# Which DRAM rows go to which partition: x and the output of a pre-LN block dealt four rows to a partition in four groups, in place of sixteen to a partition

## The chip, the cores and the metric

The kernel runs on one core of one Trainium2 chip. Its time is the device time in microseconds (us) of one execution. Engines are named as in the profile: PE is TensorE (matmuls; PEld its weight loads), DVE is VectorE, ACT is ScalarE, POOL is GpSimd, and SP is SyncE, whose queue (SPq) issues every DMA of this kernel. A core's DMAs are spread over 16 DMA engines.

## The reference

A transformer block with layer norms ahead of its two halves: linear attention with 32 heads of 16, then a dense layer with ReLU. S = 2048 rows, D = 512, Dff = 1792, all in bf16. Cut to what matters:

```python
def _A_ref(x, wqkv, wo):                       # 32 heads of 16
    q, k, v = split_heads(x @ wqkv)
    phi = lambda t: jnp.where(t > 0, t + 1, jnp.exp(t)) + 1e-6
    pq, pk = phi(q), phi(k)
    kv  = jnp.einsum("bhsd,bhse->bhde", pk, v)      # sum over all rows s
    z   = jnp.einsum("bhsd->bhd", pk)               # sum over all rows s
    num = jnp.einsum("bhqd,bhde->bhqe", pq, kv)
    den = jnp.einsum("bhqd,bhd->bhq", pq, z)[..., None] + 1e-6
    return join_heads(num / den) @ wo

def _B_ref(x, w1, w2):
    return jnp.maximum(x @ w1, 0) @ w2

h  = x + _A_ref(_layernorm(x), wqkv, wo)
h2 = h + _B_ref(_layernorm(h), w1, w2)
```

Every step works on each row by itself, but for `kv` and `z`, which are sums over all rows. No step looks at the order of the rows.

## The kernel before, in words

The 2048 rows stand on 128 partitions, 16 rows to each: the tile `x_nat` is [128, 16, 512], and its middle index t (0 to 15) is called a row tile here. Row tile t holds one row of every partition. Four row tiles make a chunk of 512 columns for the transposed operands (`CT` = 4, `NCH` = 4 chunks).

Which row of x is on which partition is said in one place, line 94, by the view `x_v = xf.rearrange("(p t) d -> p t d", p=P)`: partition p holds rows 16p to 16p + 15. Line 95 gives the output the same view, `of_v`. Three small functions use them:

- `op_lx(t, n)` (L200, its DMA is L201) loads n row tiles from t on: for each partition n rows of 1 KB, contiguous in DRAM. One such DMA is 128 KB for n = 1, 256 KB for n = 2 and 512 KB for n = 4.
- `load_d` (L203, its DMA is L204) loads the weights; `op_lk` loads two of the four blocks of wk (256 KB), `op_l1` two of the four blocks of w1 (896 KB).
- `op_fd(t, k, w)` (L527, its DMA is L529) stores row tile t of the result, 128 KB, from one of the four buffers of `o_t`; the last row tile is stored in three pieces of 32 KB, 64 KB and 32 KB.

The order of all work is written out by hand in the string `ORDER`: some 540 words such as `lx.4.2`, each of which calls `op_lx(4, 2)`. Each engine, and the SP queue, runs its instructions in the order in which these words emit them. The loads at the start stand there in the order lx.0.1, lx.2.1, lx.1.1, lx.3.1, lk.0.2, lx.4.2, lk.2.2, lx.6.2, lx.8.4, lx.12.4.

The words around the start are these. `S.t` (L222) takes the statistics of row tile t on DVE as soon as its x has landed; `A` (L223) and `R` (ACT, L228 and L229) make mean and 1/std of them; `N.t` (DVE, L247) writes the normalized row tile into `h_nat`. `T` and `E` transpose a row tile by PE (L266) and copy it into `lnT` on ACT (L276); later row tiles are transposed by DMA, `X.t` (L287). `K.t` (PE, L295) multiplies `lnT` by wk; `F` (ACT exp, L313), `U` (ACT ReLU, L316), `M` (DVE, L320) and `D` (DVE, L323) turn the product into phi(k), in the tile `pk_lo` for t = 0 and 1 and in `at` for the others. `G.t` (PE, L347) adds the row tile's share of ln(x) transposed times phi(k), from which `kv` is made, into four PSUM banks. `Q` (PE, L303) makes q. `warm` (L215) are matmuls on zeros ahead of the first real work.

After the sums over all rows are complete comes the long part: `dn` and `dt` make 1/den (`dt` by DMA transposes, L464), `h` (PE, L478) the attention output, `p` (PE, L494) the product with w1, `f` (PE, L514) that with w2, `fo` (DVE, L522) the final sum into `o_t`, and `fd` stores it.

On DVE the words after the first statistics run ... S.6, M.0.1, N.5, N.4, S.7, D.0.1, M.1.1 ...: an engine that waits for its next word's input does not pass it by.

Of the kernel before, what the change touches and what calls it, by code (L numbers as in the profile page):

```python
# [56 lines left out]
def kernel(  # L57
# [10 lines left out]
    nc = tc.nc  # L68
    P = 128
    xf = A_x.flatten_outer_dims()  # L70
    of = out.flatten_outer_dims()
# [6 lines left out]
    CT = CW // P  # L78
# [7 lines left out]
    NO = 4  # L86
# [4 lines left out]

    ctx.enter_context(tc.manual_schedule())

    x_v = xf.rearrange("(p t) d -> p t d", p=P)
    of_v = of.rearrange("(p t) d -> p t d", p=P)
    wqkv_v = A_wqkv.rearrange("(k p) n -> p k n", p=P)
    wo_v = A_wo.rearrange("(k p) n -> p k n", p=P)
    w1_v = B_w1.rearrange("(k p) n -> p k n", p=P)
# [2 lines left out]
    x_nat = big.tile([P, NT, D], BF16, name="x_nat")  # L101
# [38 lines left out]
    o_t = gT  # L140
# [57 lines left out]


    def op_lx(t, n):  # L200
        nc.sync.dma_start(out=x_nat[:, t : t + n, :], in_=x_v[:, t : t + n, :])  # L201

    def load_d(dst, src, k, n):  # L203
        nc.sync.dma_start(out=dst[:, k : k + n, :], in_=src[:, k : k + n, :])  # L204
# [321 lines left out]

    def op_fd(t, k=0, w=KD):  # L527
        cols = slice(k * P, (k + w) * P)
        nc.sync.dma_start(out=of_v[:, t, cols], in_=o_t[:, t % NO, cols])  # L529

    ops = {k[3:]: v for k, v in locals().items() if k.startswith("op_")}
    for word in ORDER.split():
# [32 lines left out]
```

## Time and profile before

| | |
|---|---|
| time, median of 3 runs | 170.41 us (170.3 to 171.33) |
| profiled execution, its own time | 172.11 us |
| its span, first to last instruction | 170.4 us |
| granted TensorE clock | 1.000 |
| busy: PE, DVE, ACT, POOL | 162.6, 106.0, 62.8, 4.8 us |
| moved by DMA | 15.87 MB in 32234 packets |
| HBM read, written | 7.86 MB, 2.10 MB |

The profile is one execution, recorded by the hardware profiler; times in it count from the span's start. Busy time is the time in which an engine executes something; in "idle before" the profile names what an engine waited for. The chain of waits follows the work that ended last back to the start, at each step to what released it. The DMA share is the busy time of the 16 DMA engines' packets over 16 times the window, and can pass 1 where packets overlap on an engine. A DMA's time to landing runs from its issue to the last byte's arrival.

### The profile page before, as it was taken

How to read it: one execution, taken by the hardware profiler on the slowest of the kernel's cores; microseconds unless marked ns; L12 is line 12 of the kernel's file. 1: busy time of each engine (PE TensorE's matmuls, PEld its weight loads, DVE VectorE, ACT ScalarE, POOL GpSimd, SP SyncE). 2: the span in 40 equal slices, each digit the busy share in tenths (PEclk: the TensorE clock that was granted, in tenths of full speed). 3: DMA queues.
4: the chain of work that ended last, by engine and by line, in shares of the span. 5: the costliest groups of instructions: out<-in, count | busy, mean ns of one | idle time of the engine just before them, and what ended most of it. 6: DMA issues, size and time to landing. Idle time of an engine off the chain costs nothing.

```text
span 170.4 us, 2280 instructions
## 1 busy us (share of the span) xinstructions
PE 162.6 (95%) x859; PEld 75.4 (44%) x859; DVE 106.0 (62%) x208; ACT 62.8 (37%) x94; POOL 4.8 (3%) x21
## 2 busy tenths in 40 slices
PE   7679989999989999999999999999999999999993
PEld 2234434445534355444444444444444444444552
DVE  3969999896768999736673983860453060315251
ACT  3768776882978857272000202034001002030000
POOL 7400000000000000000000000000000000000000
PEclk9999999999999999999999999999999999999999
DMA  4956555793353555457252142114000020000202
GB/s 125 278 213 149 99 96 123 221 392 95 73 56 62 103 93 209 88 157 185 49 82 62 20 103 62 31 36 91 0 31 0 0 92 4 31 0 19 81 31 85
DMA packets 32234, 15.87 MB, mean 93 GB/s; under 512 B 24800, under 2 KB 31200, under 8 KB 32224
## 3 DMA queue, kind: packets, MB, share of 16 engines
q1 hardware_dynamic: 32224, 15.74, 36.6%
q8 instruction: 6, 0.10, 0.2%
q14 instruction: 4, 0.03, 0.1%
HBM read 7.86 MB, written 2.10 MB: 58 GB/s over the span
## 4 chain that ended last, share of the span: by engine, by line
PE 81%; DMA 7%; DVE 5%; SPq 3%; issue 1%; ACT 1%; DVEq 0%
PE bk L494 28%; PE bk L514 28%; PE bk L478 8%; PE bk L347 6%; PE bk L303 6%; PE bk L295 4%; DMA x_nat<-in_A_x_dram 4%; DMA lnT<-h_nat 2%; DVE st L222 2%; SPq L464 2%; DMA rd<-wk_sb 1%; SPq L201 1%; DVE h_nat L247 1%; DVE eb L320 1%; PE bk L444 1%
## 5 line engine op out<-in xcount | busy, mean ns | idle before, releaser
L514 PE MATMUL bk<-w_sb,at 128*128 128x512 bf16 (+2 forms) x252 | 51.7, 355 | 0.0
L494 PE MATMUL bk<-lnT,w_sb 128*128 128x512 bf16 x224 | 51.6, 379 | 0.0
L500 ACT ACTIVATE at<-bk 128x1024 bf16<-128x1024 f32 x12 | 12.3, 1022 | 67.9 <-PE bk L494 67.9
L514 PEld LDWEIGHTS <-at 128*128 128x128 bf16 x252 | 23.6, 98 | 25.2
L505 DVE TENSOR_SCALAR at<-bk 128x1024 bf16<-128x1024 f32 x16 | 19.4, 1220 | 23.6 <-PE bk L494 23.6
L494 PEld LDWEIGHTS <-w_sb 128*128 128x128 bf16 x224 | 21.8, 98 | 26.1
L522 DVE SCALAR_TENSOR_TENSOR gT<-bk,rstd,h_nat 128x512 bf16<-128x512 f32 (+2 forms) x18 | 12.1, 685 | 18.3 <-PE bk L514 18.2
L313 ACT ACTIVATE eb<-bk 128x1024 bf16<-128x1024 f32 (+1 forms) x18 | 16.6, 928 | 4.5 <-PE bk L295 3.1
L295 PE MATMUL bk<-wk_sb,lnT 128*128 128x512 bf16 x64 | 15.5, 379 | 1.3 <-DMA wk_sb<-in_A_wqkv_dram 0.8
L316 ACT ACTIVATE rb<-bk 128x1024 bf16<-128x1024 f32 (+1 forms) x17 | 15.5, 924 | 1.6 <-PE bk L295 0.8
L478 PE MATMUL bk<-m_sb,pqs 128*128 128x512 bf16 x64 | 15.5, 380 | 0.5 <-DVE pqs L468 0.5
L303 PE MATMUL bk<-lnT,wq_sb 128*128 128x512 bf16 x64 | 15.3, 379 | 0.0
L484 DVE TENSOR_TENSOR h_nat<-bk,x_nat 128x512 bf16<-128x512 f32 x16 | 10.8, 684 | 6.4 <-PE bk L478 5.6
L347 PE MATMUL bk<-at,h_nat 128*128 128x512 bf16 x56 | 13.4, 379 | 0.0
L222 DVE BATCH_NORM_STATS2 st<-x_nat 128x6 f32<-128x512 bf16 x16 | 10.8, 685 | 3.5 <-DMA x_nat<-in_A_x_dram 3.5
L224 DVE BATCH_NORM_STATS2 st<-h_nat 128x6 f32<-128x512 bf16 x16 | 10.5, 684 | 0.1
L295 PEld LDWEIGHTS <-lnT 128*128 128x128 bf16 x64 | 6.0, 98 | 9.0 <-DMA lnT<-h_nat 1.4
L478 PEld LDWEIGHTS <-pqs 128*128 128x128 bf16 x64 | 5.9, 98 | 9.0 <-DVE pqs L468 2.4
L347 PEld LDWEIGHTS <-h_nat 128*128 128x128 bf16 x64 | 6.1, 97 | 8.3 <-issue 1.3
L303 PEld LDWEIGHTS <-wq_sb 128*128 128x128 bf16 x64 | 6.1, 98 | 6.8
L457 ACT ACTIVATE wk_sb<-ld 128x1024 bf16<-128x1024 f32 x8 | 8.2, 1051 | 1.7 <-DMA rd<-wk_sb 1.6
L468 DVE TENSOR_TENSOR pqs<-pqT,rd 128x1024 bf16<-128x1024 bf16 x8 | 5.2, 687 | 5.7 <-DMA rd<-wk_sb 5.7
(53 smaller groups left out, 86.2 us busy)
## 6 DMA issues: line engine op xcount, KB each, us to landing
w_sb<-in_B_w_dram SPq DMA_DIRECT2D x4, 896.0 KB, 5.3
out_dram<-gT SPq DMA_DIRECT2D x15, 128.0 KB, 1.9
x_nat<-in_A_x_dram SPq DMA_DIRECT2D x2, 512.0 KB, 7.5
x_nat<-in_A_x_dram SPq DMA_DIRECT2D x4, 128.0 KB, 2.4
wk_sb<-in_A_wqkv_dram SPq DMA_DIRECT2D x2, 256.0 KB, 4.0
x_nat<-in_A_x_dram SPq DMA_DIRECT2D x2, 256.0 KB, 5.1
wq_sb<-in_A_wqkv_dram SPq DMA_DIRECT2D x2, 256.0 KB, 3.0
wv_sb<-in_A_wqkv_dram SPq DMA_DIRECT2D x2, 256.0 KB, 7.0
```

The lines of the kernel that those rows point to most:

```text
L222: op_S = lambda t: nc.vector.bn_stats(out=st[:, t, :], in_=x_nat[:, t, :])
L295: nc.tensor.matmul(bk[:, b, :], lhsT=lnT[c][:, kd, j * P : (j + 1) * P], rhs=wk_sb[:, kd, :], start=(kd == 0), stop=(kd == KD - 1),)
L303: nc.tensor.matmul(bk[:, b, :], lhsT=wq_sb[:, kd, j * P : (j + 1) * P], rhs=lnT[c][:, kd, :], start=(kd == 0), stop=(kd == KD - 1),)
L313: nc.scalar.activation(out=buf(eb, kind, i, n), in_=bank(at_bank[kind, i], n), func=ACT.Exp)
L316: nc.scalar.activation(out=buf(rb, kind, i, n), in_=bank(at_bank[kind, i], n), func=ACT.Relu)
L347: nc.tensor.matmul(bk[:, KD + kd, :], lhsT=ln_nat[:, t, kd * P : (kd + 1) * P], rhs=pk(t)[:, 0, :], start=(t == 0), stop=(t == NT - 1),)
L478: nc.tensor.matmul(bk[:, b, :], lhsT=pqs[:, (c * KD + jb) % NQ, j * P : (j + 1) * P], rhs=m_sb[:, jb, :], start=(jb == 0), stop=(jb == KD ...
L494: nc.tensor.matmul(bk[:, b, cols], lhsT=w1_sb[:, kd, f * P : (f + 1) * P], rhs=lnT[c][:, kd, cols], start=(kd == 0), stop=(kd == KD - 1),)
L500: nc.scalar.activation(out=acts[c % 2][:, f : f + n, :], in_=bank(at_bank["p", c, f], n), func=ACT.Relu)
L505: nc.vector.tensor_scalar(out=acts[c % 2][:, f : f + n, :], in0=bank(at_bank["p", c, f], n), scalar1=0.0, scalar2=None, op0=ALU.max,)
L514: nc.tensor.matmul(bk[:, b, 0 : w * P], lhsT=acts[c % 2][:, f, j * P : (j + 1) * P], rhs=w2_sb[:, f, k * P : (k + w) * P], start=(f == 0), ...
L522: nc.vector.scalar_tensor_tensor(out=o_t[:, t % NO, cols], in0=bk[:, at_bank["f", t, k], 0 : w * P], scalar=rstd2[:, t : t + 1], in1=h_nat ...
```

## The change

The views of x and of the output split the rows into four groups of 512 first, and give each partition four consecutive rows of each group: partition p holds rows 512a + 4p to 512a + 4p + 3 for a = 0 to 3. Group a fills the four row tiles 4a to 4a + 3 of `x_nat`. `op_lx` and `op_fd` split their index t into the group and the row within it. No load crosses a group's edge. `ORDER` and everything else stay as they are.

```diff
-    x_v = xf.rearrange("(p t) d -> p t d", p=P)
-    of_v = of.rearrange("(p t) d -> p t d", p=P)
+    x_v = xf.rearrange("(a p t) d -> p a t d", p=P, t=CT)
+    of_v = of.rearrange("(a p t) d -> p a t d", p=P, t=CT)
...
     def op_lx(t, n):
-        nc.sync.dma_start(out=x_nat[:, t : t + n, :], in_=x_v[:, t : t + n, :])
+        a, j = divmod(t, CT)
+        nc.sync.dma_start(out=x_nat[:, t : t + n, :], in_=x_v[:, a, j : j + n, :])
...
     def op_fd(t, k=0, w=KD):
         cols = slice(k * P, (k + w) * P)
-        nc.sync.dma_start(out=of_v[:, t, cols], in_=o_t[:, t % NO, cols])
+        nc.sync.dma_start(out=of_v[:, t // CT, t % CT, cols], in_=o_t[:, t % NO, cols])
```

In DRAM the pieces that one load or store takes for two neighbouring partitions lie 16 rows (16 KB) apart before, and 4 rows (4 KB) apart after; lx.8.4 and lx.12.4 then each read 512 KB that are contiguous as a whole.

## The prediction

> **What bounds the kernel now.** I read the chain of waits in order of time first, because it says which stage a change in the loads could move at all. Columns: start in us, length in us, what.
>
> ```profile
> 4.12 6.20 DMA x_nat<-in_A_x_dram
> 10.32 0.02 issue
> 10.34 0.04 DVE st L222
> ...
> 18.82 3.40 DMA lnT<-h_nat
> 22.22 0.05 issue
> 22.27 1.04 PE bk L295 x4
> ...
> 167.53 0.03 issue
> 167.56 0.35 DVE gT L522
> ```
>
> The chain has three parts. Up to 10.3 us it is a load of x: the one issued at 4.12, which by ORDER is lx.6.2 (the SP queue issues lx.0.1, lx.2.1, lx.1.1, lx.3.1, lk.0.2, lx.4.2, lk.2.2, lx.6.2, lx.8.4, lx.12.4). From 10.34 to 18.82 it is VectorE. From 22.27 to 167.5 it is TensorE, and then the last store. Next the table of windows for the stages after the loads (us of window, then its length and the busy time of PE, PEld, DVE, ACT, POOL, then clock, DMA share, GB/s):
>
> ```profile
> 10.34:18.82 8.48, 7.41 (x35) 3.20 (x34) 8.48 (x27) 6.51 (x14) 0.00 (x0) 1.00 0.51 127
> 18.82:22.27 3.45, 2.89 (x15) 1.10 (x13) 3.38 (x10) 2.73 (x5) 0.00 (x0) 1.00 0.60 113
> 22.27:44.00 21.73, 21.73 (x129) 10.28 (x130) 19.36 (x34) 14.49 (x19) 0.00 (x0) 1.00 0.59 176
> 44.00:51.06 7.06, 6.55 (x57) 3.36 (x55) 4.72 (x8) 5.92 (x7) 0.00 (x0) 1.00 0.55 78
> 51.06:167.56 116.50, 116.45 (x592) 54.25 (x592) 63.75 (x112) 27.25 (x36) 0.00 (x0) 1.00 0.27 65
> ```
>
> TensorE is busy for 21.73 + 6.55 + 116.45 = 144.73 of the 145.29 us from 22.27 to 167.56, at a granted clock of 1.00. It has 0.56 us of idle time there, none of it behind a load of x. So a faster or slower transfer after 22 us is hidden, and whatever this change does to the time it does before 22.27 us, or after 167.56 us in the last store. The waits that end between 5 and 24 us are these (total us, times, longest):
>
> ```profile
> DVE st L222 <- DMA x_nat<-in_A_x_dram: 1.7, 2, 1.3
> ...
> PE bk L347 <- DVE pk_lo L323: 1.1, 1, 1.1
> ...
> PE bk L266 <- DVE h_nat L247: 0.8, 2, 0.4
> PE bk L295 <- DMA wk_sb<-in_A_wqkv_dram: 0.8, 1, 0.8
> PE bk L295 <- DMA lnT<-h_nat: 0.6, 1, 0.6
> ```
>
> TensorE idles for 1.1 + 0.8 + 0.8 + 0.6 = 3.3 us here. That is the ceiling for any gain: with all of it gone the span would be 170.4 - 3.3 = 167.1 us. VectorE's share of the loads is 1.7 us, in two pieces, which the timeline places:
>
> ```profile
> 7.21 0.69 DVE L222 BATCH_NORM_STATS2 st<-x_nat 128x6 f32<-128x512 bf16 x1 [0.37 <-DMA x_nat<-in_A_x_dram]
> ...
> 10.34 0.69 DVE L222 BATCH_NORM_STATS2 st<-x_nat 128x6 f32<-128x512 bf16 x1 [1.31 <-DMA x_nat<-in_A_x_dram]
> ```
>
> The first is S.4 waiting for lx.4.2, the second S.6 waiting for lx.6.2. Behind S.6 on VectorE stand M.0.1, N.5, N.4, S.7 and D.0.1, which writes the pk_lo that the first G on TensorE waits for, the 1.1 us above.
>
> **The change, part by part.** No instruction is added, removed or reordered. Each lx still fills the same tile with n rows of 1 KB per partition, contiguous in DRAM before and after, and each fd still writes 1 KB (or less) per partition. What moves is the distance in DRAM from one partition's piece to the next: 16 rows, 16 KB, before; 4 rows, 4 KB, after. The first four loads then share one stretch of 512 KB instead of being spread over 2 MB, and lx.8.4 and lx.12.4 become one contiguous 512 KB each. The sixteen rows of a partition are other rows than before, but every step works row by row or sums over all rows, so no other engine's work changes. Its cost is nothing and needs no cover.
>
> *Stores.* The page's issue groups, with the loads beside them (count, KB each, median us from issue to landing), and min/median/max of all 18 stores:
>
> ```profile
> out_dram<-gT SPq DMA_DIRECT2D x15, 128.0 KB, 1.9
> x_nat<-in_A_x_dram SPq DMA_DIRECT2D x2, 512.0 KB, 7.5
> x_nat<-in_A_x_dram SPq DMA_DIRECT2D x4, 128.0 KB, 2.4
> wk_sb<-in_A_wqkv_dram SPq DMA_DIRECT2D x2, 256.0 KB, 4.0
> x_nat<-in_A_x_dram SPq DMA_DIRECT2D x2, 256.0 KB, 5.1
> ```
>
> ```profile
> DMA to landing us min/median/max: 1.5/1.8/2.1
> ```
>
> Only the last store is on the path; the others land in about 2 us under TensorE's 116 us. If a pitch of 4 KB changes a store's landing, the end moves by at most the spread of this row, 0.6 us either way. I take zero: a landing that stays within 1.5 to 2.1 us over stores of 32 to 128 KB is mostly a fixed delay.
>
> *Loads.* The page's 128 KB loads take 2.4 us while the 256 KB ones take 5.1, so the question is what the queue does in between. The windows of half a microsecond (last two columns: DMA share, GB/s):
>
> ```profile
> 6.50:7.00 0.50, 0.50 (x8) 0.41 (x9) 0.34 (x2) 0.23 (x2) 0.00 (x0) 1.00 1.11 309
> 7.00:7.50 0.50, 0.50 (x6) 0.23 (x4) 0.29 (x1) 0.47 (x3) 0.00 (x0) 1.00 1.51 242
> 7.50:8.00 0.50, 0.13 (x1) 0.00 (x0) 0.50 (x2) 0.50 (x2) 0.00 (x0) 1.00 0.89 188
> 8.00:8.50 0.50, 0.12 (x1) 0.10 (x1) 0.50 (x2) 0.37 (x1) 0.00 (x0) 1.00 0.60 213
> 8.50:9.00 0.50, 0.50 (x6) 0.28 (x5) 0.50 (x3) 0.00 (x0) 0.00 (x0) 1.00 0.78 287
> 9.00:9.50 0.50, 0.50 (x7) 0.27 (x5) 0.03 (x1) 0.49 (x1) 0.00 (x0) 1.00 1.01 365
> ```
>
> Here lies the dip. With a queue full of x, the rate falls from 309 to 188 GB/s and comes back to 365. At 7.00 the engines' share is 1.51 for 242 GB/s against 1.01 for 365, so a byte took 2.3 times as long: the packets themselves waited. Against 365 GB/s the five windows lack 56 + 123 + 177 + 152 + 78 = 586 GB/s, times 0.5 us is 293 KB, which at 365 GB/s is 0.80 us. That is what lx.6.2, and S.6 behind it, would gain if the dip went.
>
> Does the pitch make the dip? For it: this is the stretch in which only x is left in the queue. Against it: the load of w1, whose rows are contiguous, begins with a dip as well.
>
> ```profile
> 31.50:32.00 0.50, 0.50 (x5) 0.20 (x3) 0.50 (x1) 0.02 (x1) 0.00 (x0) 1.00 0.91 115
> 32.00:32.50 0.50, 0.50 (x4) 0.26 (x3) 0.50 (x2) 0.50 (x1) 0.00 (x0) 1.00 0.54 165
> 32.50:33.00 0.50, 0.50 (x4) 0.22 (x3) 0.50 (x2) 0.50 (x2) 0.00 (x0) 1.00 1.04 423
> ```
>
> It lacks 308 + 258 = 566 GB/s against 423, times 0.5 us, or 0.67 us at that rate. But it lies at the start of a load out of an idle queue, while x's dip comes in mid-stream, and behind it the contiguous load runs at 423, x at 365. That suggests that contiguous rows are served at least as well once running.
>
> The bounds for the loads: upward, all of VectorE's 1.7 us of waiting, and with it TensorE's 0.8 us for wk_sb, which stands in the same queue; these overlap in part, so between 1.7 and 2.5 us. Downward, three new dips like w1's, one where each of the second, third and fourth stretches is opened, 3 x 0.67 = 2.0 us. I take the value in between whose row is this kernel's own x load, 0.80 us: lx.6.2 lands at about 9.5, S.6 starts with it, VectorE's run of 8.48 us from 10.34 to 18.82 moves up as a block, and TensorE's 1.1 us wait for pk_lo shrinks to 0.3. What is late next is VectorE itself, which in its window above is busy for 8.48 of 8.48 us.
>
> Weighed against this: the Trainium skill, DMA: Bandwidth & Descriptors, section "Latency and other measured facts", lists copies whose row pitch in HBM is a large power of two: 207 GB/s at 512 KiB, 164 at 2 MiB, 103 at 4 MiB, against 214 with a padded pitch, and it calls the mechanism inferred. By it a pitch of 16 KB should cost nothing and the time would stay; the trace's 365 GB/s at 9.0 us with x alone agrees, its 188 at 7.5 us doesn't, and no run here shows a larger pitch.
>
> **The sum.** Against the profiled execution: span 170.4 - 0.8 (loads) + 0 (stores) = 169.6 us. That execution took 172.11 us, 1.7 more than its span, while the runs without a profile have their median at 170.41 (170.3 to 171.33), close to the span; so I put the difference on the median: 170.41 - 0.8 = 169.6 us.
>
> **The rivals.**
>
> *All load waits go.* If the packets of x were slow because of the pitch throughout, and not in the dip alone, all ten loads move up, S.4 and S.6 find their rows there and the 1.7 us go; with half of TensorE's 0.8 us for wk_sb, 2.1 us: 168.3 us. For it: x never reaches the 423 GB/s that w1 does. Against it: 365 GB/s at 9.0 us with x alone leaves little to speed up.
>
> *Nothing moves.* The dip belongs to the moment (queues filling, engines out of step) and not to the pitch; it returns, lx.6.2 lands at 10.3 and the time is 170.4, give or take the 0.6 us of the last store. The rule above gives the same. This is also the time if the change, which alters addresses alone, does nothing that the memory notices.
>
> *Slower: each new stretch opens with a dip.* Before, lx.0.1 touches all of x's 2 MB. After, lx.4.2, lx.8.4 and lx.12.4 each open 512 KB of their own, and w1 shows what opening costs: 0.67 us. The three fall in mid-queue ahead of S.6 and S.9: 2.0 us later, 172.4 us. It decides against me as soon as lx.6.2 lands after 12.0 us, that is 1.7 us later than now. Against it: lx.0.1, which opens x out of an idle queue, lands in about the 2.4 us of its group.
>
> **How the numbers follow.** Forecast (most of the dip goes) 35%, all waits go 25%, nothing moves 15%, slower 25%. One per cent, 1.7 us, is about what a measurement of this kernel can tell from no change: below 168.7 is faster, above 172.1 slower. Faster takes the second case and the good end of the first, 0.29. Slower takes nine tenths of the last, 0.23, since with two dips instead of three it stays under 172.1. The rest, 0.48, is within 1%. The likeliest case alone spans 168.9 to 170.4. The range has to take in the cases of both signs, 168.3 and 172.4, with some tenths for the stores: 167.9 to 172.7.
>
> **What would show it.** In the changed kernel's profile: the windows from 6.5 to 9 us without a value under 250 GB/s, S.6's wait for x_nat at 0.3 to 0.6 us instead of 1.31, the chain still passing from a load to VectorE to TensorE, TensorE solid from about 21.5 us, and stores landing at 1.5 to 2.1 us. The forecast is wrong if lx.6.2 lands within 0.3 us of 10.3, if a dip stands at the start of lx.4.2 or lx.8.4 instead, or if TensorE shows a wait for a load that it has not now.

## The result

| | before | changed |
|---|---|---|
| time, median of 17 runs each | 170.65 us (170.27 to 172.83) | 171.84 us (170.97 to 172.72) |
| ratio, 95% interval | | 1.0059 (1.0039 to 1.0080) |
| profiled execution: own time, span | 172.11, 170.4 us | 170.97, 169.3 us |

The changed kernel is 0.6 per cent slower, 1.0 us, where 0.8 us faster was forecast. Yet its profiled span is 1.1 us shorter than the one shown of before. Both are true, and how they fit is the main thing to learn here. Of all executions below, one of e10's was in a slower state (span 172.0 us) and is left out of its mean.

The chain of waits of the changed kernel, in order of time (start us, length us, what):

```profile
0.80 2.39 DMA x_nat<-in_A_x_dram
3.19 0.02 issue
3.21 1.29 DVE st L223 x2
...
17.64 3.38 DMA lnT<-h_nat
21.03 0.05 issue
21.07 1.04 PE bk L296 x4
...
166.39 0.03 issue
166.41 0.35 DVE gT L523
```

TensorE's solid part begins at 21.07 us, 1.20 us sooner than in the profile of before, and the end comes 1.1 us sooner. From there to the last instruction of the chain it is 145.3 us in both. The timeline at the start, VectorE's statistics with their waits:

```profile
3.21 1.29 DVE L223 BATCH_NORM_STATS2 st<-x_nat 128x6 f32<-128x512 bf16 x2 [1.99 <-DMA x_nat<-in_A_x_dram]
...
7.46 0.69 DVE L223 BATCH_NORM_STATS2 st<-x_nat 128x6 f32<-128x512 bf16 x1 [0.47 <-DMA x_nat<-in_A_x_dram]
```

S.6 waits for nothing now (1.31 us in the profile of before), but S.4's wait has grown from 0.37 to 0.47, and S.0's from 1.80 to 1.99. The windows of half a microsecond (the last two columns are DMA share and GB/s) say which loads are served faster and which slower:

```profile
5.50:6.00 0.50, 0.50 (x5) 0.34 (x5) 0.50 (x3) 0.47 (x3) 0.43 (x2) 1.00 0.42 129
6.00:6.50 0.50, 0.50 (x4) 0.11 (x1) 0.50 (x2) 0.42 (x3) 0.15 (x1) 1.00 0.75 252
6.50:7.00 0.50, 0.50 (x6) 0.27 (x6) 0.50 (x3) 0.40 (x1) 0.00 (x0) 1.00 1.10 371
7.00:7.50 0.50, 0.50 (x7) 0.38 (x7) 0.04 (x1) 0.44 (x3) 0.00 (x0) 1.00 1.07 391
7.50:8.00 0.50, 0.29 (x2) 0.01 (x1) 0.50 (x1) 0.50 (x3) 0.00 (x0) 1.00 1.06 404
8.00:8.50 0.50, 0.38 (x2) 0.10 (x1) 0.50 (x3) 0.50 (x2) 0.00 (x0) 1.00 1.01 410
```

The dip at 6.5 to 9 us is gone: 371 to 410 GB/s where the profile of before had 188 to 309. In its place there is one at 5.5 to 6.5 us, 129 and 252 GB/s, where before had 342 and 365. The issue groups (KB each, median us from issue to landing) show the same by size:

```profile
out_dram<-gT SPq DMA_DIRECT2D x15, 128.0 KB, 2.0
x_nat<-in_A_x_dram SPq DMA_DIRECT2D x2, 512.0 KB, 5.8
x_nat<-in_A_x_dram SPq DMA_DIRECT2D x4, 128.0 KB, 2.5
```

The contiguous loads land in 5.8 us instead of 7.5, the first ones a little later than before, the stores as before.

### The profile page after: what moved, and what is told of

Read it like the earlier page. It is cut to its first block, busy times and chain, and to the rows that moved or that the text cites. A ratio compares the mean times of both kernels' runs of the same rounds, so it can differ in the third digit from the quotient of the medians.

```text
span 169.3 us, 2280 instructions
## 1 busy us (share of the span) xinstructions
PE 163.5 (97%) x859; PEld 75.6 (45%) x859; DVE 105.8 (63%) x208; ACT 63.0 (37%) x94; POOL 4.7 (3%) x21
## 4 chain that ended last, share of the span: by engine, by line
PE 82%; DVE 7%; DMA 5%; issue 1%; SPq 1%; ACT 1%; DVEq 0%
PE bk L495 29%; PE bk L515 29%; PE bk L479 9%; PE bk L348 6%; PE bk L304 6%; PE bk L296 4%; DVE st L223 3%; DMA lnT<-h_nat 2%; DVE h_nat L248 2%; DMA rd<-wk_sb 2%; SPq L465 1%; DMA x_nat<-in_A_x_dram 1%; DVE eb L321 1%; PE bk L445 1%; DVE mv L224 1%
```

## The experiments

For every execution from here on, and for the 17 of the changed kernel above, the span is on record beside the time. The time is longer than the span by at least 1.66 us in each of them, profiled or not; for the 17 runs of the changed kernel the median of the difference is 1.74 us and the largest 2.9. Spans, which leave this difference out, are compared below, always with those of the kernel before on the same chip. The means rest on 12 executions each, but for e7 (9), e8 (6), e10 (11), e11 (7) and e12 (6).

**Which profile to believe, and which half of the change.** e1 is the kernel before and e2 the changed kernel, unedited. e3 has the new view for the loads alone, e4 for the stores alone:

```diff
 e3
+    x_v = xf.rearrange("(a p t) d -> p a t d", p=P, t=CT)
     of_v = of.rearrange("(p t) d -> p t d", p=P)
 e4
     x_v = xf.rearrange("(p t) d -> p t d", p=P)
+    of_v = of.rearrange("(a p t) d -> p a t d", p=P, t=CT)
```

> The kernel before, unchanged, to see whether its profile was a usual execution. Theory P (the profiled execution was an unusually late one: it took 172.11 us where the median of the kernel is 170.65): time equal to before within 0.3 per cent, spans mostly 168.7 to 169.3 us, the wait of VectorE for x in a usual profile under 0.5 us after the first arrival, TensorE solid from about 21 us. Theory Q (the profile is usual and the execution with the profile only carries a fixed extra 1.7 us): spans of 170.2 to 170.6 us in nearly all executions.

> The changed kernel again, as the yardstick for the next two on the same chip. Both theories: 1.003 to 1.009 of before, spans 169.4 to 170.5 us. Its first profile came from its fastest execution (170.97 us), so this one should show TensorE solid later than 21.07 us, at 21.3 to 22 us.

> The new view for the loads of x alone; the stores keep the old one, so the rows of the output come out in another order. Theory L (the loads carry the loss: the new stretches open with slow packets): 1.004 to 1.008, as the whole change. Theory S (the stores carry it: 1 KB pieces 4 KB apart are written later or disturb other transfers): 1.000 within 0.002.

> The new view for the stores alone; the loads keep the old one, so the rows of the output come out in another order. Theory L: 1.000 within 0.002. Theory S: 1.004 to 1.008, with the last store landing some 1 us later or TensorE idle after 90 us, where the stores begin.

| | median us | ratio, 95% interval | mean span us |
|---|---|---|---|
| e1, the kernel before | 170.71 | 0.9984 (0.9955 to 1.0013) | 168.94 |
| e2, the changed kernel | 171.83 | 1.0041 (1.0009 to 1.0073) | 169.58 |
| e3, loads alone | 171.56 | 1.0023 (0.9991 to 1.0056) | 169.64 |
| e4, stores alone | 170.74 | 0.9988 (0.9953 to 1.0024) | 169.09 |

Theory P holds. Of 47 executions of the kernel before on this chip, 44 had a span under 170.0 us and two reached 170.4. The execution whose profile the prediction was built on was one of the latest there are. A usual one is e1's. Its chain of waits:

```profile
3.65 4.47 DMA wk_sb<-in_A_wqkv_dram
8.12 0.04 issue
...
17.51 3.42 DMA lnT<-h_nat
...
20.97 1.04 PE bk L295 x4
```

In this usual execution the chain leaves the loads by lk.2.2, the second load of wk, which lands at 8.12 us, and not by lx.6.2. Its statistics' waits, and its windows from 5.5 us on:

```profile
3.04 1.29 DVE L222 BATCH_NORM_STATS2 st<-x_nat 128x6 f32<-128x512 bf16 x2 [1.82 <-DMA x_nat<-in_A_x_dram]
...
8.82 0.70 DVE L222 BATCH_NORM_STATS2 st<-x_nat 128x6 f32<-128x512 bf16 x1 [0.17 <-DMA x_nat<-in_A_x_dram]
```

```profile
5.50:6.00 0.50, 0.50 (x6) 0.46 (x5) 0.50 (x2) 0.47 (x3) 0.38 (x3) 1.00 0.95 336
6.00:6.50 0.50, 0.50 (x4) 0.03 (x2) 0.50 (x3) 0.41 (x2) 0.27 (x1) 1.00 1.06 322
6.50:7.00 0.50, 0.50 (x8) 0.50 (x8) 0.50 (x3) 0.40 (x2) 0.00 (x0) 1.00 0.91 291
7.00:7.50 0.50, 0.50 (x7) 0.29 (x5) 0.48 (x2) 0.47 (x3) 0.00 (x0) 1.00 1.42 285
7.50:8.00 0.50, 0.19 (x1) 0.00 (x0) 0.50 (x2) 0.50 (x2) 0.00 (x0) 1.00 1.14 213
8.00:8.50 0.50, 0.34 (x2) 0.19 (x2) 0.50 (x3) 0.36 (x1) 0.00 (x0) 1.00 0.61 225
```

The dip is there in a usual execution too, 213 and 225 GB/s. But S.6 waits 0.17 us behind it and S.4 nothing, and TensorE is solid from 20.97 us, sooner than in the changed kernel's profile, which itself was its best of 17. The 1.31 us that the prediction meant to shorten is mostly not there in a usual execution. e2's profile fell on the fastest of its 12 executions (span 168.9 us), and TensorE is solid from 20.99 us there, not from 21.3 to 22 as expected: single profiles of the two kernels overlap, and only the means tell them apart.

For the halves, the intervals of the ratios are as wide as the effect; the spans decide. With a spread of 0.3 to 0.7 us, the mean of 12 is uncertain by 0.1 to 0.2. e3 stands with e2 (169.64 and 169.58), e4 with e1 (169.09 and 168.94): theory L, the loads carry it.

**Which loads.** e5 to e7 use both views, chosen by row tile: e5 the new one for `t >= 4`, e6 for `t < 4`, e7 for `t >= 8`, e11 (run later) for `4 <= t < 8`. e8 and e12 are other full layouts.

```diff
+    x_g = xf.rearrange("(a p t) d -> p a t d", p=P, t=CT)
...
+        a, j = divmod(t, CT)
+        src = x_g[:, a, j : j + n, :] if t >= 4 else x_v[:, t : t + n, :]
+        nc.sync.dma_start(out=x_nat[:, t : t + n, :], in_=src)
 e12
+    x_v = xf.rearrange("(a p t) d -> p a t d", p=P, t=2 * CT)
+    of_v = of.rearrange("(a p t) d -> p a t d", p=P, t=2 * CT)
```

> The first four loads (row tiles 0 to 3) and the stores as before; lx.4.2, lx.6.2, lx.8.4 and lx.12.4 with the new view. Some rows of x are so loaded twice and others not at all. Theory A (the loss comes from the first four loads, which land 0.2 us later each): time of before within 0.002, spans near 168.9 us. Theory B (the loss comes from lx.4.2 and lx.6.2, which open a stretch of their own, with the dip at 5.5 to 6.5 us): 1.003 to 1.006, spans near 169.6 us, DMA rate under 250 GB/s somewhere between 5 and 7 us, and S.0 at 3.0 us.

> The first four loads with the new view; all others and the stores as before. Some rows of x are loaded twice and others not at all. Theory A: 1.003 to 1.006, spans near 169.6 us. Theory B: at most 1.002, spans of 168.9 to 169.2 us (the 0.2 us by which S.0 starts later is all that is left). Both: S.0 at 3.2 us, and the dip of 188 to 290 GB/s at 6.5 to 9 us as before.

> Only lx.8.4 and lx.12.4, the two contiguous ones, with the new view. Some rows of x are loaded twice and others not at all. Both theories: not slower than before. If the dip at 6.5 to 9 us is made by these two loads' pitch, it goes here (no window under 280 GB/s from 7 to 9.5 us), lx.12.4 lands at 11.3 to 12 us instead of 12.5 to 13, and the late executions of before (spans over 169.4 us) become rarer: mean span 168.6 to 168.9 us, ratio 0.997 to 1.000. If the dip belongs to the moment, it stays, and so does everything else.

> A full kernel with a third layout for loads and stores: row tiles 0 to 7 take eight rows to a partition from the first 1024 rows (pitch 8 KB), row tiles 8 to 11 and 12 to 15 four rows to a partition each, contiguous. Theory B: lx.4.2 opens nothing of its own here, since lx.0.1 has spread over the same 1 MB; time of before or a little less, 0.997 to 1.001. Theory A: half of the loss remains at half the stretch, 1.001 to 1.004, with S.0 at 3.1 us.

> Only lx.4.2 and lx.6.2 with the new view; the other loads and the stores as before. Some rows of x are loaded twice and others not at all. It completes the table of the three parts alone: first four loads 169.3 us mean span, last two 169.8 us, all but the first four 169.2 us, before 168.95 us. Theory C (what stands behind lx.6.2 decides): as before, 168.8 to 169.1 us. Theory D (a narrow stretch of its own): 169.3 to 169.6 us.

> The whole change at half its step: two groups of 1024 rows with eight rows to a partition, pitch 8 KB, loads and stores; a full kernel. If the loss grows steadily from a pitch of 16 KB to one of 4 KB: spans of 169.2 to 169.5 us. If 8 KB is worse than both, as the mixed layout with 170.3 us hints: 169.8 to 170.4 us, with lx.0.1 landing at 3.15 us and lx.6.2 after 9.5 us.

In this table pitch is the distance of neighbouring partitions' pieces, for row tiles 0 to 3, 4 to 7 and 8 to 15; a span of before stands beside each. The last columns are one profile each, in us: where S.0 starts, and how long lx.4.2 and lx.6.2 took from issue to landing.

| | pitch KB | ratio, 95% interval | mean span, before | S.0 | lx.4.2, lx.6.2 |
|---|---|---|---|---|---|
| e1 | 16, 16, 16 | 0.9984 (0.9955 to 1.0013) | 168.94, 169.01 | 3.04 | 3.2, 4.7 |
| e2 | 4, 4, 4 | 1.0041 (1.0009 to 1.0073) | 169.58, 169.01 | 3.23 | 3.8, 4.9 |
| e3 | 4, 4, 4 | 1.0023 (0.9991 to 1.0056) | 169.64, 169.01 | 3.25 | 4.4, 5.4 |
| e6 | 4, 16, 16 | 1.0017 (0.9994 to 1.0039) | 169.30, 168.95 | 3.21 | 4.0, 5.0 |
| e5 | 16, 4, 4 | 1.0022 (1.0000 to 1.0044) | 169.23, 168.95 | 3.03 | 3.6, 5.3 |
| e7 | 16, 16, 4 | 1.0044 (1.0017 to 1.0072) | 169.76, 168.95 | 3.02 | 3.4, 5.7 |
| e11 | 16, 4, 16 | 1.0067 (1.0030 to 1.0103) | 170.29, 168.94 | 3.00 | 4.0, 6.5 |
| e8 | 8, 8, 4 | 1.0090 (1.0060 to 1.0120) | 170.32, 168.95 | 3.19 | 4.6, 6.3 |
| e12 | 8, 8, 8 | 1.0121 (1.0086 to 1.0157) | 170.98, 168.94 | 3.19 | 5.0, 6.6 |

Neither theory A nor theory B comes out as the whole. S.0 starts 0.2 us later exactly where the first four loads do not have the pitch of 16 KB, as A says, and that is more than half of e6's 0.35 us. lx.4.2 lands in 3.2 to 3.4 us where the loads up to it have that pitch, and in 3.6 to 5.0 us elsewhere, as B says. These are single profiles, though: in the first profile of the kernel before, with a pitch of 16 KB throughout, lx.4.2 and lx.6.2 took 4.0 and 6.2 us. And the parts do not add: e7 and e11, which change the least, cost 0.8 and 1.4 us, more than the whole change, and 8 KB is worse than both 16 and 4; for e8 and e11, too, both theories were wrong. In e7 the time goes to lx.6.2, as its wait of S.6 shows (first line below). In e11 that wait is longer still (second line), but the chain leaves the loads by lk.2.2 there, which lands only at 9.00 us:

```profile
9.80 0.69 DVE L225 BATCH_NORM_STATS2 st<-x_nat 128x6 f32<-128x512 bf16 x1 [1.18 <-DMA x_nat<-in_A_x_dram]
```

```profile
10.62 0.69 DVE L225 BATCH_NORM_STATS2 st<-x_nat 128x6 f32<-128x512 bf16 x1 [1.61 <-DMA x_nat<-in_A_x_dram]
```

Both expectations for e7 were wrong: it is slower. A load of one pitch that is still on its way when loads of another come in behind it seems to be hurt by them. That was not taken further and stays a guess.

e6 and e7 also say which loads' pitch the dip at 6.5 to 9 us follows. Two windows and the 512 KB loads of e6, where lx.8.4 and lx.12.4 are laid out as before, and then the same of e7, where they are contiguous:

```profile
7.50:8.00 0.50, 0.33 (x2) 0.05 (x1) 0.50 (x2) 0.50 (x3) 0.00 (x0) 1.00 1.05 369
8.00:8.50 0.50, 0.07 (x1) 0.07 (x1) 0.50 (x2) 0.50 (x2) 0.00 (x0) 1.00 1.19 416
x_nat<-in_A_x_dram SPq DMA_DIRECT2D x2, 512.0 KB, 6.1
```

```profile
7.50:8.00 0.50, 0.50 (x3) 0.17 (x2) 0.50 (x2) 0.50 (x2) 0.00 (x0) 1.00 1.02 266
8.00:8.50 0.50, 0.50 (x7) 0.33 (x6) 0.50 (x3) 0.37 (x2) 0.00 (x0) 1.00 1.05 266
x_nat<-in_A_x_dram SPq DMA_DIRECT2D x2, 512.0 KB, 6.8
```

This is not what was expected. In e6 the dip was to stay, and it is gone, with one at 5.5 to 7 us in its place (195, 195 and 150 GB/s), as in the changed kernel. In e7 it was to go if the pitch of these two loads made it, and it stays. So the dip moves with the layout of the first four loads, which have landed before it, more than with that of the loads it falls into. The latter count as well: e5 and e11 differ only in lx.8.4 and lx.12.4, which take 6.4 us in e5, where they are contiguous, and 7.6 in e11. Why the first loads should matter so is open; these kernels also read some rows twice.

**Does the traffic behind take the bandwidth?** e9 (changed) and e10 (before) hold lx.8.4 and what follows it back until VectorE has done S.3:

```diff
-... T.0.6 S.3 N.2 ...
+... T.0.6 S.3 hold.8 N.2 ...
+    op_hold = lambda t: nc.vector.memset(x_nat[:, t, 0:1], 0.0)
```

> The changed kernel, with lx.8.4 and lx.12.4 held back until VectorE has done S.3 (a write of one column to row tile 8 at that place makes the load wait; it costs VectorE about 0.06 us), so that their packets begin at about 7.2 us instead of 6.5. Theory C (the two contiguous loads run at 400 GB/s and take bandwidth from the last packets of lx.6.2 and lk.2.2 ahead of them): lx.6.2 lands at 8.3 to 8.7 us and the spans come back to 168.9 to 169.3 us, ratio 1.000 to 1.003. Theory D (packets of the early loads are slower in the narrow stretch, whatever stands behind them): spans stay at 169.6 to 170.0 us, ratio 1.004 to 1.007.

> The kernel before with the same hold. Theory C: the late executions become rarer, mean span 168.5 to 168.8 us instead of 169.0, ratio 0.997 to 1.000. Theory D: unchanged, mean span 168.9 to 169.1 us. If the two loads now come too late for S.9 and S.13, both are wrong and VectorE waits for x after 11 us.

e9: 1.0047 (1.0018 to 1.0076), mean span 169.59 us, that of before 168.94. e10: 0.9984 (0.9958 to 1.0009), mean span 168.76. e9 does not change, and its dip at 5.5 us stays (154 GB/s): theory C falls for the changed kernel, whose loss it was to explain. For the kernel before, e10 lies in theory C's range and not in theory D's: 0.18 us less than the kernel before, about as much as the two means leave uncertain. Its ratio is the one that e1, the same kernel without the hold, has too, so no gain is shown.

**Is it the first reading of a stretch?** This was the prediction's rival on the slow side: a stretch that wasn't read before opens with slow packets. e13 reads a little of x's upper 1.5 MB early on ScalarE's queue, e14, as a control, a little of the part that the first four loads read anyway, e15 a little of wk in the kernel before, e16 both in the changed kernel:

```diff
+    scratch = big.tile([P, 1, 32], BF16, name="scratch")
+    def op_touch():
+        nc.scalar.dma_start(out=scratch[:, 0, :],
+            in_=xf[CW:, :].rearrange("(p t) d -> p t d", p=P)[:, 0, 0:32])
-const table lx.0.1 ...
+touch const table lx.0.1 ...
```

> The changed kernel with one small extra load ahead of everything, on ScalarE's queue: 128 pieces of 64 bytes, 12 KB apart, out of the 1.5 MB of x that the first four loads do not read. Nothing uses what it loads. Theory O (the dip of 129 to 266 GB/s at 5.5 to 6.5 us comes from the first reads of a new stretch of x): the dip goes, both windows over 290 GB/s, spans of 169.0 to 169.4 us, ratio 1.000 to 1.003. Theory I (it comes from the mixture of the two streams, x and wk, in the queue, whatever was read before): dip and spans stay, 169.5 to 170.1 us, ratio 1.004 to 1.008.

> The control: the same small load, but out of the 512 KB of x that the first four loads read anyway. Both theories: as the changed kernel or up to 0.2 us later for the extra packets, spans of 169.5 to 170.2 us, dip at 5.5 to 6.5 us as there.

> The kernel before with the same kind of small load out of wk's columns of wqkv. Theory O, carried over to the weights: the dip of 145 to 164 GB/s at 4.0 to 4.5 us, where lk.0.2 begins, goes (over 230 GB/s), lk.2.2 lands 0.2 to 0.3 us sooner and the spans are 168.5 to 168.8 us, ratio 0.997 to 0.999. Theory I: dip and time stay, ratio 0.999 to 1.002.

> The changed kernel with both small loads, x's upper 1.5 MB and wk. Theory O: no window under 250 GB/s between 2.5 and 9 us, spans of 168.6 to 169.1 us, ratio 0.997 to 1.001. Theory I: as the changed kernel, 1.004 to 1.008.

e13 and its control e14 come out alike: 1.0041 (1.0018 to 1.0065) and 1.0035 (1.0010 to 1.0060). The windows at the dip, first of e13, then of e14:

```profile
5.50:6.00 0.50, 0.24 (x5) 0.24 (x5) 0.50 (x3) 0.47 (x3) 0.43 (x2) 1.00 1.22 231
6.00:6.50 0.50, 0.37 (x4) 0.04 (x1) 0.50 (x2) 0.47 (x3) 0.21 (x1) 1.00 0.83 158
```

```profile
5.50:6.00 0.50, 0.25 (x5) 0.25 (x5) 0.50 (x3) 0.47 (x3) 0.43 (x2) 1.00 0.83 197
6.00:6.50 0.50, 0.37 (x4) 0.03 (x1) 0.50 (x2) 0.47 (x3) 0.21 (x1) 1.00 0.81 246
```

The dip stays, with a little of the stretch read before or not. e15 keeps its own at 4.0 to 4.5 us (162 GB/s, 145 in e1) and is no faster: 1.0009 (0.9986 to 1.0032). e16 lies in between at 1.0026 (1.0000 to 1.0053), its windows at 5.5 to 6.5 us at 252 and 268 GB/s, and the kernel is still on the slow side. Theory O finds no support, but these loads touch only 8 KB of the stretch. The stronger evidence is e8 and e12: there lx.0.1 to lx.3.1 have read from the same 1 MB as lx.4.2, which so opens nothing new in the theory's sense, and yet lx.4.2 takes 4.6 and 5.0 us.

**x alone.** e17 (changed) and e18 (before) leave out the two loads of wk, so that only x is in the queue at the start:

```diff
-lk.0.2 ... lk.2.2
...
         make_identity(nc, ident[:])
+        nc.gpsimd.memset(wk_sb[:], 0.0)
```

> The changed kernel without its two loads of wk (512 KB): wk_sb is filled with zeros by GpSimd instead, so k is zero. The queue at the start holds x alone. Theory I (the loss comes from x in the new layout and wk being read side by side): no window under 250 GB/s from 2.5 us to the end of the loads, and the span is not longer than that of e18, within 0.2 us. Theory X (x's own pieces of 2 KB at a pitch of 4 KB are read more slowly): a dip under 270 GB/s remains where lx.4.2 begins, and the span is 0.4 to 0.9 us longer than that of e18.

> The kernel before without its two loads of wk, as the yardstick for e17. Both theories: no dip at 4.0 to 4.5 us if that one belongs to wk; the one where lx.8.4 comes in stays, 190 to 290 GB/s over some 2 us, now at 5 to 7.5 us; spans of 167.5 to 168.8 us, since TensorE and the loads of x behind wk come sooner.

The issue groups of e17, then of e18:

```profile
x_nat<-in_A_x_dram SPq DMA_DIRECT2D x2, 512.0 KB, 6.4
x_nat<-in_A_x_dram SPq DMA_DIRECT2D x4, 128.0 KB, 2.6
x_nat<-in_A_x_dram SPq DMA_DIRECT2D x2, 256.0 KB, 4.3
```

```profile
x_nat<-in_A_x_dram SPq DMA_DIRECT2D x2, 512.0 KB, 7.6
x_nat<-in_A_x_dram SPq DMA_DIRECT2D x4, 128.0 KB, 2.5
x_nat<-in_A_x_dram SPq DMA_DIRECT2D x2, 256.0 KB, 3.3
```

Without wk beside it, the effect of the whole layout stands clear, and it has two signs. The loads of 2 KB to a partition land 1.0 us later at a pitch of 4 KB (4.3 against 3.3), and the loads of 4 KB to a partition 1.2 us sooner when they are contiguous (6.4 against 7.6). Windows of e17, then of e18, where the first difference and the second lie:

```profile
4.00:4.50 0.50, 0.50 (x2) 0.15 (x1) 0.50 (x2) 0.00 (x0) 0.43 (x3) 1.00 1.01 203
4.50:5.00 0.50, 0.50 (x2) 0.15 (x1) 0.50 (x3) 0.30 (x2) 0.43 (x3) 1.00 1.16 246
...
8.00:8.50 0.50, 0.50 (x6) 0.23 (x4) 0.50 (x2) 0.50 (x2) 0.00 (x0) 1.00 1.02 418
```

```profile
4.00:4.50 0.50, 0.50 (x3) 0.17 (x2) 0.48 (x3) 0.05 (x1) 0.43 (x3) 1.00 0.95 309
4.50:5.00 0.50, 0.50 (x3) 0.05 (x1) 0.50 (x1) 0.45 (x2) 0.43 (x3) 1.00 0.95 318
...
8.00:8.50 0.50, 0.40 (x5) 0.22 (x4) 0.50 (x2) 0.50 (x2) 0.10 (x1) 1.00 0.79 246
```

Theory X is right about the loads: the dip belongs to x's own loads, not to a mixture with wk. These two runs change all loads at once, so they don't say whether a load's own pitch or that of the loads ahead of it sets its rate. Theory X is wrong about the time. Mean spans are 168.97 us in e17 and 168.69 in e18, 0.28 us apart and not 0.4 to 0.9, because in neither does a statistic wait for any load but the first. And the first explains nearly all of the 0.28: S.0 starts at 3.26 us in e17 and at 3.02 in e18.

With this the loss can be put together in part. The later first load costs 0.2 to 0.3 us (e17 against e18). e2 and e3 have mean spans 0.64 and 0.70 us above e1's, so some 0.4 us are left, and these appear only with wk in the queue. A likely carrier is the wait of S.4 or S.6 for a later lx.4.2 or lx.6.2: 0.47 us in the changed kernel's first profile, 0.27 in e2's, 0.59 in e3's, against 0.17 in e1's and none in e4's. That is not shown. e14, the changed kernel with a small load more, has no such wait; e2's profiled execution was no later than e1's (168.9 and 169.0 us) in spite of its longer wait; and in e3, as in e1, the chain leaves the loads by lk.2.2:

```profile
3.64 4.77 DMA wk_sb<-in_A_wqkv_dram
8.41 0.04 issue
```

It lands at 8.41 us there and at 8.12 in e1. Which of the loads ends last changes from one execution to the next.

## Why the prediction was wrong

*Where the time is made.* Right. TensorE solid to the end, stores landing in about 2 us, e4 at the time of before: all that the change does, it does at the start, through the loads.

*The dip and the pitch.* Right in the outcome, but not shown as a mechanism. The layout of x does make the dip from 6.5 to 9 us: it goes with the change, and e18 shows it without wk beside it, 246 GB/s against 418 in e17 at 8 us. That was partly luck. The queue did not hold x alone there, as the prediction has it: lk.2.2 was on its way until 8.35 us (issued at 3.65, 4.7 us to landing). And the contiguous loads do not remove the dip: in e7 it stays with them (266 GB/s), and in e6 it is gone without them (369 and 416). It was weighed against the Trainium skill (DMA: Bandwidth & Descriptors, section "Latency and other measured facts"), whose row pitches start at 512 KiB with hardly a loss. Read downwards, which the page itself does not do, that gave no effect here; these runs differ, with mean spans of 168.94, 170.98 and 169.58 us at 16, 8 and 4 KB, and the measurement decides.

*"I put the difference on the median."* This is the first step that failed; it turned the forecast gain into none. The prediction saw a profiled execution of 172.11 us beside a median of 170.41 and a highest run of 171.33, and took the 1.7 us for something that the profile adds. But at least 1.66 us stand between span and time in every execution, so a median of 170.41 means a span near 168.7. The profiled one was simply 1.5 us later than usual (170.4 against e1's mean of 168.94), and what was late in it was lx.6.2. The forecast removed 0.8 us of a wait of 1.31 that is 0.17 us or nothing in a usual execution. The rest of that chain, from S.6 through VectorE's block to the wait for pk_lo, was followed from a wait that is usually not there.

*What the changed loads cost.* This is the second step that failed; it hid the loss. The prediction let the early loads gain or stay, and took from the contiguous load of w1 that contiguous rows are served at least as well. In the changed kernel lx.8.4 and lx.12.4 do land sooner (5.8 us, against 7.0 in e1), but nothing waits for them. The loads that VectorE does wait for are not contiguous after the change but 1 and 2 KB out of every 4, and for those the row of w1 said nothing. They land 0.2 us (lx.0.1) and 0.5 to 1.2 us (lx.4.2, e2 and e3 against e1 and e4, 3.8 and 4.4 us against 3.2 and 3.3) later. The sum had no term for that. The first load's 0.2 to 0.3 us are shown to reach the time; which wait carries the other 0.4 us stays open.

*The rival on the slow side.* It had the sign, and a dip did appear where lx.4.2 begins, but the runs speak against its mechanism: lx.8.4 opens its stretch at 371 to 404 GB/s, reading a little of the stretch beforehand changes nothing, and e8 and e12, where lx.4.2 opens no stretch of its own, lose more. Its 2.0 us were two to three times the loss.

*What would show it.* Most of the signs named there came true in the changed kernel's profile: no window under 250 GB/s from 6.5 to 9 us, TensorE solid before 21.5 us, stores as before, and S.6's wait even gone where 0.3 to 0.6 us were named. The kernel is slower all the same, for they had been compared with a late execution. One sign of being wrong came true as well: the dip at the start of lx.4.2.

## What to carry to other kernels

Before building on a profile, set the profiled execution's own time beside the other runs of the same kernel: if it lies above their highest, its longest wait is the first suspect for what made it late, and a gain taken from that wait is a gain on one execution. For a change of layout, price each load by the wait that its own arrival ends, not by the load that speeds up most: here 1.2 us gained on loads that nobody waits for stood against 0.2 us lost on the first, which everybody waits for. And don't carry a rate from one load to another: here the size of the pieces, their pitch and the layout of the loads ahead all made a difference, and not in one direction.

## What the runs showed of the hardware that was not expected

- At pitches of a few KB the order isn't monotonic: whole layouts with 16, 4 and 8 KB between partitions gave mean spans of 168.94, 169.58 and 170.98 us, in the order of the landing of lx.4.2 in one profile each (3.2, 3.8 and 5.0 us).
- With x alone in the queue and all its loads at one pitch, the pieces of 4 KB come in at 246 GB/s (8.0 to 8.5 us) at a pitch of 16 KB where contiguous ones reach 418, and with pieces of 2 KB it is the other way round: in the two windows where they come in, from 4 to 5 us, 309 and 318 GB/s at a pitch of 16 KB, 203 and 246 at 4 KB (e18 and e17). It is not the load's own pitch alone: in the same window e6 has 416 GB/s with the 4 KB pieces at 16 KB, behind first loads at 4 KB, and e7 has 266 with them contiguous, behind first loads at 16 KB.
- Changing the pitch of the two loads in the middle of the queue, e11, costs 1.4 us, more than changing all. Why the memory serves these patterns so differently was not settled: the profile shows rates and landings, not which part of the memory a packet goes to. The dip at lx.4.2 comes without the traffic behind it (e9) and without wk beside x (e17, 242 GB/s from 5 to 6 us), and a first reading of its stretch is an unlikely cause (e13 and e14, e8 and e12).
